# Feed-forward and output weights kept in SBUF for the 256-query passes of a two-layer attention and MLP kernel

## Chip, cores and metric

The kernel runs on one core of one Trainium2 chip. The metric is device time in microseconds (us) of one execution; the profile's span leaves out about 2 us of it.

## The reference, cut to what matters

```python
# S = 2048 tokens, D = 512, H = 32 heads of Dh = 16, F = 1792; bf16 in and out
def _A_ref(x, wqkv, wo):      # attention
    ...                       # q, k, v = x @ wqkv, by head
    scores = jnp.einsum("bhqd,bhkd->bhqk", q, k) * scale
    p = _softmax(scores, axis=-1)
    o = jnp.einsum("bhqk,bhkd->bhqd", p, v)
    return ... @ wo
def _B_ref(x, w1, w2):        # feed-forward
    h = _silu(jnp.einsum("bsd,df->bsf", x, w1))
    return jnp.einsum("bsf,fd->bsd", h, w2)

x = x + _A_ref(_layernorm(x), A_wqkv, A_wo)     # layer 0
x = x + _B_ref(_layernorm(x), B_w1, B_w2)
x = x + _A_ref(_layernorm(x), A_wqkv, A_wo)     # layer 1, the same weights
x = x + _B_ref(_layernorm(x), B_w1, B_w2)
```

Both layers use the same weights. `w1` is 1.8 MB (14 tiles of 128 KB), `wo` is 0.5 MB, `w2` is 1.8 MB and stays in SBUF throughout.

## The kernel before

The foreground is attention: scores on TensorE, exponentials mostly on ScalarE (a fourth of the blocks on VectorE and GpSimd instead), and their product with V on TensorE. Everything else (projections, layer norm, feed-forward) is cut into small pieces of "background", which a planner places at build time wherever its own model of the engines says TensorE has room. So TensorE's program is a fixed order in which background matmuls stand between score matmuls. If a background matmul waits, the scores behind it wait, and then the exponentials wait.

Queries go in passes. Layer 0 has four passes of 512 queries (`L, u` = 0, 0 to 3). Layer 1 has two passes of 512 (1, 0 and 1, 1) and four of 256 (1, 2 to 1, 5); the code calls the latter halved. The feed-forward of a pass runs in the background of the next one. The last one, of (1, 5), runs alone at the end and is called the tail.

Every load goes to one DMA queue, that of SyncE (SP), in program order. An instruction there that waits for a buffer or for its input holds back all that follow (below, a transpose that waited 3.4 us for its input held back a weight tile):

```python
def load(out, in_):
    nc.sync.dma_start(out, in_)
    if bg.model:
        bg.model.dma(1)               # charges the planner's model of the queue
...
w1pool = ctx.enter_context(tc.tile_pool(name="w1pool", bufs=3))
...
class W1:                             # one per pass: streams w1, two tiles ahead
    def __init__(self):
        self.tiles = {}
        for ft in range(2):
            self.load(ft)
    def load(self, ft):
        if ft < FT:                   # FT = 14
            self.tiles[ft] = w1pool.tile([P, CT, P], BF16, name="w1", tag="w1")
            load(self.tiles[ft][:], B_w1.rearrange(...)[:, :, ft * P : (ft + 1) * P])
    def get(self, ft):
        self.load(ft + 2)
        return self.tiles.pop(ft)
...
def h_pair(w1, ft, fT, i):            # 256-query passes: two tiles into one PSUM bank
    for k in range(2):
        yield part(pe=0.43, held=k > 0)
        if k == 0:
            ps = bank("h_ps")
        w = w1.get(ft + k)
        for ct in range(CT):
            nc.tensor.matmul(ps[...], lhsT=w[:, ct, :], rhs=fT[:, i : i + 2, ct, :], ...)
...
def load_wo():                        # wo shares the buffer of the hidden activations
    wo[0] = hpool.tile([P, FT, 512], BF16, name="wo", tag="hT")
    load(wo[0][:, 0:CT, :], A_wo.rearrange("(ct p) e -> p ct e", p=P))
...
def ffn(L, u):
    ...
    w1 = W1()
    yield part(need=("fT", L, u))     # fT: the normalized input, transposed by DMA
    hT = hpool.tile([P, FT, 512], BF16, name="hT", tag="hT")
    ...                               # h = silu(fT x w1) into hT, then hT x w2 into x
    load_wo()                         # for the next output projection
```

The output weights are thus loaded again after every feed-forward, because the hidden activations `hT` overwrite them, and the load can start only when the last reader of `hT` has finished. Shortly before the tail, `load_w1_tail` puts all 14 tiles of `w1` into slots that are free by then.

The softmax here doesn't subtract the row's maximum and nothing guards it: scores larger than these inputs give would overflow.

Of the kernel before, what the change touches and what calls it, by code (L numbers as in the profile page):

```python
# [20 lines left out]
BF16 = mybir.dt.bfloat16  # L21
# [206 lines left out]
def kernel(  # L228
# [10 lines left out]
    nc = tc.nc  # L239
# [4 lines left out]
    P = 128  # L244
# [3 lines left out]
    CT = D // P  # L248
    NC = S // 512
    FT = F // P  # L250
    NG = H // 8
    NKT = S // P
# [22 lines left out]
    ORDER = (*range(1, NG), 0)  # L275
# [14 lines left out]
    def halved(L, u):  # L290
        return L == 1 and u >= 2
# [17 lines left out]
    w1pool = ctx.enter_context(tc.tile_pool(name="w1pool", bufs=3))  # L309
# [9 lines left out]
    wo = {}  # L319
# [13 lines left out]
# [3 lines that stand above are left out]
            bg.model.dma(1)  # L336
# [42 lines left out]
    partial = {}  # L379

    def kslot(n, shape, dtype, name):

        return kpool.tile(shape, dtype, name=name, tag=f"K{n}")

    def xslot(n, name):

        return xtpool.tile([P, 4, CT, P], BF16, name=name, tag=f"X{n}")
# [252 lines left out]
    def load_wo():  # L640

        wo[0] = hpool.tile([P, FT, 512], BF16, name="wo", tag="hT")
        load(wo[0][:, 0:CT, :], A_wo.rearrange("(ct p) e -> p ct e", p=P))
# [37 lines left out]
        tt = 4 * c + i  # L681
        load(of[tt * P : (tt + 1) * P, :] if L == 1 else x1[c][:, i, :], x_sb[c][:, i, :])

    class W1:


        def __init__(self):
            self.tiles = {}
            for ft in range(2):
                self.load(ft)  # L690

        def load(self, ft):
            if ft < FT:
                self.tiles[ft] = w1pool.tile([P, CT, P], BF16, name="w1", tag="w1")
                load(
                    self.tiles[ft][:],
                    B_w1.rearrange("(ct p) f -> p ct f", p=P)[:, :, ft * P : (ft + 1) * P],
                )

        def get(self, ft):  # L700
            self.load(ft + 2)
            return self.tiles.pop(ft)

    def h_whole(w1, ft, fT):
        w = w1.get(ft)
        return (yield from mm4("h_ps", lambda ct: w[:, ct, :], lambda ct: fT[:, :, ct, :], out=0))

    def h_pair(w1, ft, fT, i):

        for k in range(2):  # L710
            yield part(pe=0.43, held=k > 0)
            if k == 0:
                ps = bank("h_ps")
            w = w1.get(ft + k)
            for ct in range(CT):
                nc.tensor.matmul(  # L716
                    ps[:, 256 * k : 256 * (k + 1)].rearrange("p (t q) -> p t q", q=P),
                    lhsT=w[:, ct, :],
                    rhs=fT[:, i : i + 2, ct, :],
                    start=(ct == 0),  # L720
                    stop=(ct == CT - 1),
                )
        yield part(0, held=True)
        return ps

    def ffn(L, u):
        c, tiles = tiles_of(L, u)
        if (L, u) < (1, 3):
            nxt = (c + 1) % NC
            load_x(nxt, x1[nxt] if (L, u) >= (0, NC - 1) else None)  # L730
        w1 = W1()
        yield part(need=("fT", L, u))
        fT = fTs.pop((L, u))
        hT = hpool.tile([P, FT, 512], BF16, name="hT", tag="hT")
        n = 2 if halved(L, u) else 1
        for ft in range(0, FT, n):
            if n == 1:
                h_ps = yield from h_whole(w1, ft, fT)
            else:
                h_ps = yield from h_pair(w1, ft, fT, tiles[0])  # L740
            t_sb = tpool.tile([P, 512], FP32, name="t_sb", tag="t")
            silu_tanh(h_ps, t_sb[:])
            yield part(0.6, held=True)
            silu_mul(
                hT[:, ft : ft + n, 0 : 512 // n],
                *(x.rearrange("p (n q) -> p n q", n=n) for x in (h_ps, t_sb[:])),
            )
        for k, i in enumerate(tiles):
            yield part(pe=0.43)
            y_ps = bank("f_ps")  # L750
            for ft in range(FT):
                nc.tensor.matmul(  # L752
                    y_ps,
                    lhsT=hT[:, ft, k * P : (k + 1) * P],
                    rhs=w2_sb[:, ft, :],
                    start=(ft == 0),
                    stop=(ft == FT - 1),
                )
                if ft % 2 == 1 and ft < FT - 1:
                    yield part(pe=0.43, held=True)  # L760
            yield part(0.6, held=True)
            ffn_out(L, c, i, y_ps)
            if L == 0 and i % 2 == 1:
                bg.add_side(None, ln_pair(c, i - 1))
        if L == 0:
            bg.add_side(("ln", 1, c), ln_attn(1, c))
        load_wo()

    def run(gen):

# [10 lines left out]
        for i in range(n):  # L781
            nc.tensor.matmul(ps, lhsT=ident[:], rhs=w_qkv[:, i % CT, 0:D], start=True, stop=True)  # L782

    w1_tail = {}

    def load_w1_tail():

        w1 = B_w1.rearrange("(ct p) f -> p ct f", p=P)
        rest = xslot(3, "w1_rest")
        for n in range(4):  # L790
            if n < 3:
                some = kslot(1 + n, [P, CT, 512], BF16, "w1_tail")
                nc.sync.dma_start(some[:], w1[:, :, 512 * n : 512 * (n + 1)])
            for ft in range(4 * n, min(4 * n + 4, FT)):
                if n < 3:
                    w1_tail[ft] = some[:, :, P * (ft % 4) : P * (ft % 4 + 1)]
                else:
                    w1_tail[ft] = rest[:, ft % 4, :, :]
                    nc.sync.dma_start(w1_tail[ft], w1[:, :, P * ft : P * (ft + 1)])

    def tail(L, u):

        c, tiles = tiles_of(L, u)
        aT = xslot(2, "aT")
        fT = xslot(L, "fT")
        ts = kslot(4, [P, 4, 256], FP32, "t_tail")
        LAG = 3
        COPY = (nc.vector.tensor_copy, nc.scalar.copy)

        def turn_tile(src, dst, copy):  # L810
            t_ps = bank("t_ps", BF16)[:, 0:512]
            for ct in range(CT):
                nc.tensor.transpose(  # L813
                    t_ps[:, ct * P : (ct + 1) * P], src[:, ct * P : (ct + 1) * P], ident[:, :]
                )
            copy(out=dst.rearrange("p c q -> p (c q)"), in_=t_ps)  # L816

        for n in range(2):
            turn_tile(attn[L, u][:, n, :], aT[:, n, :, :], COPY[n])
        for n, i in enumerate(tiles):  # L820
            run(out_add(c, i, aT[:, n, :, :]))
        warm(8)
        mv, rstd = run(ln_stats(c, tiles))
        for n, i in enumerate(tiles):
            xn = ln_apply(c, i, mv[:, n, :], rstd[:, n, :])
            turn_tile(xn, fT[:, n, :, :], COPY[1 - n])
            if n == 0:
                warm(2)

        hT = hpool.tile([P, FT, 512], BF16, name="hT", tag="hT")  # L830
        f_ps = [bank("f_ps") for _ in range(2)]

        def f_part(n, ft):
            nc.tensor.matmul(  # L834
                f_ps[n],
                lhsT=hT[:, ft, n * P : (n + 1) * P],
                rhs=w2_sb[:, ft, :],
                start=(ft == 0),
                stop=(ft == FT - 1),
            )  # L840

        for k in range(FT):
            h_ps = bank("h_ps")[:, 0:256]
            for ct in range(CT):
                nc.tensor.matmul(  # L845
                    h_ps.rearrange("p (t q) -> p t q", q=P),
                    lhsT=w1_tail[k][:, ct, :],
                    rhs=fT[:, 0:2, ct, :],
                    start=(ct == 0),
                    stop=(ct == CT - 1),  # L850
                )
            t_sb = ts[:, k % 4, :]
            silu_tanh(h_ps, t_sb)
            silu_mul(hT[:, k, 0:256], h_ps, t_sb)
            if k >= LAG:
                for n in range(2):
                    f_part(n, k - LAG)
        for n, i in enumerate(tiles):
            for ft in range(FT - LAG, FT):
                f_part(n, ft)  # L860
            ffn_out(L, c, i, f_ps[n])
# [9 lines left out]
    for g in range(NG):  # L871
        mine = [r for r in runs if r[3] == g]
        n = 0
# [24 lines left out]
    steps, pv_steps = plan()  # L898
    pv_left = {}
    for ts in pv_steps.values():  # L900
        t, k = ts[0]
        key = steps[t][0][k][0:5]
# [240 lines left out]
    with tc.manual_schedule(  # L1143
# [68 lines left out]
        for t in range(1, len(steps)):  # L1212
# [3 lines left out]
                if qc == 0:  # L1216
                    bg.ensure(("k", L, kt // 4, g))
            L, qc, pi, g, par, kt, j = a_blks[0]
            if t == len(steps) - 3 * NKT:
                load_w1_tail()  # L1220
            if kt == kts_of[L, qc, pi, g, par][0]:
                for Lq, c, gq, n in q_next.get((L, qc, pi, g, par), []):
                    bg.add(("q", Lq, c, gq, n), proj_q(Lq, c, gq), first=True)
# [17 lines left out]
            if t < D_LEAD:  # L1241
                p = p_pre[:, 3 * t + 1 : 3 * t + 4, :]
                parts = [p[:, 0:n1, :], p[:, n1 : n1 + 2, :]]
            elif n1 == 1:
                p = ppool.tile([P, 3, 512], BF16, name="p_sb", tag="p")
# [25 lines left out]
            if n1 == 2 and d_blks:  # L1271
                if t > 5 and m.free <= m.pe and bg.idle():
                    n = int((m.sd - m.pe - 2 * m.SWITCH) / m.GROUP)
# [6 lines left out]
            if not busy and m.fill_fits(FILL):  # L1280
                n = fill(FILL)
# [6 lines left out]
        t = len(steps) + 1  # L1288
# [40 lines left out]
```

## Time and profile before

| | before |
|---|---|
| median, 4 runs | 1580.38 us (1574.95 to 1582.19) |
| ScalarE (ACT) busy | 1512.2 of 1578.7 us |
| TensorE (PE) busy | 1465.1 us |
| HBM read | 33.29 MB |

The engine table of the profile of before: per engine, busy time, share of the span and instructions.

```profile
span 1578.7 us, 39884 instructions
...
PE 1465.1 (93%) x15947; PEld 536.1 (34%) x16056; DVE 1034.8 (66%) x1714; ACT 1512.2 (96%) x2185; POOL 1141.8 (72%) x1245
```

ScalarE is the bound. The Trainium skill, "Perfetto Trace Analysis", section "Identifying the Most-Contended Engine", says that for ScalarE the occupancy is also a fair measure of the distance to the roofline, and that a busy share of TensorE is not. The next view agrees: for over a millisecond ScalarE has next to no gap, while VectorE and GpSimd have slack. So the question is where its 66.5 us of idle time lie. This is the view by stretches of before (from and to, length, then busy time and instructions of each engine, granted TensorE clock, DMA share, GB/s). The bounds are start-up, middle, the stretch with the 256-query passes, and the tail.

```profile
core 0: us, PE busy (x) PEld busy (x) DVE busy (x) ACT busy (x) POOL busy (x), PEclk, DMA share, GB/s
0.00:100.00 100.00, 86.76 (x681) 28.61 (x689) 76.63 (x144) 86.74 (x125) 62.28 (x98) 0.98 0.28 77
100.00:1250.00 1150.00, 1091.98 (x10702) 363.59 (x10774) 778.71 (x1258) 1146.76 (x1657) 877.64 (x935) 1.00 0.15 33
1250.00:1549.87 299.87, 264.91 (x4422) 131.34 (x4447) 166.69 (x283) 272.15 (x390) 200.57 (x211) 0.93 0.23 51
1549.87:1579.00 29.13, 21.42 (x146) 12.59 (x148) 12.79 (x30) 6.54 (x16) 1.33 (x3) 0.94 0.03 10
```

Length less ScalarE busy gives idle time: 13.3, 3.2, 27.7 and 22.6 us. The third stretch stands out, and so does its clock of 0.93. What TensorE waited for there is the view of waits of before, cut to TensorE and this stretch (who <- for what: us in total, times, longest us):

```profile
PE y_ps L486 <- DMA wo<-in_A_wo_dram: 6.0, 2, 3.1
PE h_ps L716 <- DMA w_23318<-in_B_w_dram: 5.1, 1, 5.1
...
PE h_ps L716 <- DMA w_25071<-in_B_w_dram: 3.2, 1, 3.2
PE h_ps L716 <- DMA w_27182<-in_B_w_dram: 2.8, 1, 2.8
...
PE h_ps L716 <- DMA w_23626<-in_B_w_dram: 1.7, 1, 1.7
PE h_ps L716 <- DMA w_25379<-in_B_w_dram: 1.7, 1, 1.7
PE h_ps L716 <- DMA w_27490<-in_B_w_dram: 1.6, 1, 1.6
PE h_ps L716 <- DMA fT<-xn: 1.2, 1, 1.2
```

There are eight waits for weights of over 1 us, 22.1 us in sum: twice for `wo`, and in each of three passes for two tiles of `w1`. `wo` is late because it waits for its buffer: it was issued 1.3 us after the last matmul that read `hT`, and took 3.8 and 4.0 us to land. The tiles are late because of their place in the queue. The timeline of the DMA queue in before, around the longest wait (start, length, what was issued, how often), shows it:

```profile
1306.01 0.44 SPq L334 DMA_DIRECT2D w_22849<-in_B_w_dram  x1
1306.49 0.51 SPq L334 DMA_DIRECT2D w_22851<-in_B_w_dram  x1
1307.10 2.54 SPq L329 DMA_TRANSPOSE fT<-xn  x2
1309.75 1.69 SPq L329 DMA_TRANSPOSE ot<-oT  x1
1313.06 5.45 SPq L533 DMA_DIRECT2D QT<-q  x8
1318.63 1.19 SPq L329 DMA_TRANSPOSE ot<-oT  x1
1319.86 0.58 SPq L334 DMA_DIRECT2D w_23318<-in_B_w_dram  x1
...
1334.41 1.19 SPq L329 DMA_TRANSPOSE ot<-oT  x1
1335.69 0.53 SPq L334 DMA_DIRECT2D w_23626<-in_B_w_dram  x1
```

Tiles 1 and 2 are issued in time. Tile 3 (`w_23318`) stands behind eight query copies and two attention transposes and is issued at 1319.86; TensorE has stood still since 1317.45 and goes on at 1322.5. An issued tile of this size lands in 2.2 to 3.7 us in this stretch.

In a gap, or soon after it, the clock falls too. In the longest wait it fell at 1320.6, about 3 us into the gap. The view by stretches of before, for 9 us ahead of that wait and for the 6.8 us in which the clock was low:

```profile
1308.00:1317.00 9.00, 8.64 (x160) 4.54 (x156) 5.64 (x10) 9.00 (x15) 7.15 (x8) 1.00 0.64 89
1320.60:1327.40 6.80, 4.89 (x51) 2.55 (x52) 1.63 (x3) 2.52 (x4) 1.44 (x2) 0.50 0.43 96
```

A score matmul of 256 columns took 403 ns in the second stretch, against 271 from 1290 to 1317 us.

### The profile page before, as it was taken

What the parts mean: (1) busy time and instruction counts of PE and PEld (TensorE: products, weight loads), DVE (VectorE), ACT (ScalarE), POOL (GpSimd) and SP (SyncE); (2) the same over time, 40 slices, a digit from 0 to 9 for tenths busy, and PEclk for the clock granted to TensorE, in tenths of its full rate; (3) what the DMA queues carried; (4) which work ended last, traced back from release to release, by engine and by line L of the source; (5) the groups of instructions that cost most, each with busy time, mean ns of one, the idle gap of its engine ahead of it and who ended that gap; (6) DMA issues with size and microseconds to landing.
All of it is one profiled execution on the core that took longest, in us unless ns stands there. A gap on an engine that the chain in (4) does not pass through costs nothing. (4 is left out here: it accounts for less than half of the span.)

```text
span 1578.7 us, 39884 instructions
## 1 busy us (share of the span) xinstructions
PE 1465.1 (93%) x15947; PEld 536.1 (34%) x16056; DVE 1034.8 (66%) x1714; ACT 1512.2 (96%) x2185; POOL 1141.8 (72%) x1245
## 2 busy tenths in 40 slices
PE   7999999899989999899998999999998987889997
PEld 3222332233223333233332323322344444444444
DVE  6877676667766667666676677766676555555553
ACT  6999999999999999999999999999999988889994
POOL 2888777678867788678876777777787765667761
PEclk9999999999999999999999999999999999999999
DMA  4100022111220202201111010120122113121410
GB/s 140 31 24 2 5 38 65 28 34 25 51 55 15 46 14 53 49 18 41 34 39 31 11 32 13 43 51 24 36 51 50 24 31 79 34 61 30 91 40 19
DMA packets 168250, 61.51 MB, mean 39 GB/s; under 512 B 145536, under 2 KB 167552, under 8 KB 168064
## 3 DMA queue, kind: packets, MB, share of 16 engines
q1 hardware_dynamic: 168064, 58.96, 16.3%
q8 instruction: 125, 2.05, 0.5%
q14 instruction: 61, 0.50, 0.1%
HBM read 33.29 MB, written 4.19 MB: 24 GB/s over the span
## 5 line engine op out<-in xcount | busy, mean ns | idle before, releaser
L1186 ACT ACTIVATE p_sb<-s_ps 128x512 bf16<-128x512 f32 x2026 | 1467.9, 1107 | 12.6 <-PE d_ps L928 11.9
L1095 DVE TENSOR_SCALAR d_y<-d_ps 128x512 uint16<-128x512 f32 x1012 | 698.2, 690 | 463.5 <-PE d_ps L928 409.9
L928 PE MATMUL s_ps<-QT,KT 32*128 32x512 bf16 (+1 forms) x3852 | 641.3, 339 | 49.1 <-ACT p_sb L1186 35.3
L928 PEld LDWEIGHTS <-KT 32*128 32x128 bf16 x5120 | 199.9, 91 | 606.0 <-issue 564.9
L928 PE MATMUL d_ps<-QT,KT 32*128 32x512 bf16 (+1 forms) x1268 | 392.5, 342 | 3.1 <-DVE d_y L1095 2.5
L964 PE MATMUL o_ps<-p_sb,VA 128*32 128x512 bf16 (+1 forms) x3807 | 315.2, 346 | 7.0 <-ACT p_sb L1186 1.1
L964 PEld LDWEIGHTS <-VA 128*32 128x32 bf16 x5120 | 121.2, 96 | 138.0 <-issue 105.5
L964 PE MATMUL o_ps<-d_y,VA 128*32 128x512 f16 (+1 forms) x1268 | 154.1, 338 | 0.0
L964 PEld LDWEIGHTS <-VB 128*32 128x32 f16 x2536 | 99.6, 99 | 42.6 <-issue 0.5
L665 ACT ACTIVATE t_sb<-h_ps 128x512 f32<-128x512 f32 x105 | 90.9, 865 | 19.9 <-PE h_ps L716 16.7
L752 PE MATMUL f_ps<-w_sb,hT 128*128 128x512 bf16 x370 | 103.3, 384 | 5.7 <-issue 5.0
L668 DVE SCALAR_TENSOR_TENSOR hT<-t_sb,h_ps 128x512 bf16<-128x512 f32 x105 | 71.8, 684 | 20.0 <-ACT t_sb L665 19.0
L964 PE MATMUL o_ps<-w_qkv,zero 128*32 128x512 bf16 (+1 forms) x1356 | 73.3, 335 | 0.0
L1075 DVE CAST oT<-o_ps 128x512 bf16<-128x512 f32 (+1 forms) x80 | 45.9, 574 | 7.7 <-PE o_ps L964 7.7
L752 PEld LDWEIGHTS <-hT 128*128 128x128 bf16 x420 | 31.4, 98 | 48.4 <-issue 26.2
L419 DVE BATCH_NORM_STATS2 st<-x 128x6 f32<-128x512 bf16 x64 | 43.6, 681 | 2.0 <-DMA x<-in_A_x_dram 2.0
L430 DVE TENSOR_SCALAR xn<-x,mv,rstd 128x513 bf16<-128x513 bf16 x64 | 40.7, 650 | 2.9 <-POOL rstd L424 1.7
L964 PEld LDWEIGHTS <-zero 128*32 128x32 bf16 x1356 | 28.0, 95 | 27.1 <-issue 20.0
L486 PE MATMUL q_ps<-xnT,w_qkv 128*128 128x512 bf16 x136 | 35.9, 382 | 0.4 <-DVE q L531 0.2
L486 PE MATMUL k_ps<-xnT,w_qkv 128*128 128x512 bf16 x128 | 35.2, 386 | 1.0 <-DVE xnT L1164 0.6
L627 POOL TENSOR_TENSOR attn<-ot,rec 128x128 bf16<-128x128 bf16 (+1 forms) x61 | 31.1, 509 | 6.1 <-DVE rec L620 6.0
L486 PE MATMUL v_ps<-w_qkv,xnT 128*128 128x512 bf16 x112 | 33.0, 382 | 1.4 <-issue 0.6
(2355 smaller groups left out, 2089.5 us busy)
## 6 DMA issues: line engine op xcount, KB each, us to landing
wo<-in_A_wo_dram SPq DMA_DIRECT2D x10, 512.0 KB, 3.9
QT<-q SPq DMA_DIRECT2D x240, 16.0 KB, 1.8
x<-in_A_x_dram SPq DMA_DIRECT2D x7, 512.0 KB, 4.4
out_dram<-x SPq DMA_DIRECT2D x16, 128.0 KB, 1.8
w_sb<-in_B_w_dram SPq DMA_DIRECT2D x1, 1792.0 KB, 13.9
w_qkv<-in_A_wqkv_dram SPq DMA_DIRECT2D x3, 512.0 KB, 7.5
w_tail<-in_B_w_dram SPq DMA_DIRECT2D x3, 512.0 KB, 6.3
ot<-oT SPq DMA_TRANSPOSE x61, 2.4
```

Source lines behind the costliest of these rows:

```text
L419: nc.vector.bn_stats(st[:], x_sb[c][:, i, :])
L430: nc.vector.tensor_scalar(out=wide[:].rearrange("p (a b) -> p a b", b=19), in0=x_wide[c][:, D * i : D * (i + 1) + 1], scalar1=mv[:, 0:1], ...
L486: nc.tensor.matmul(ps.rearrange("p (t q) -> p t q", q=P) if len(r.shape) == 3 else ps, lhsT=lhs(ct), rhs=r, start=(ct == 0), stop=(ct == C ...
L627: scale(out=attn[L, qc][:, 0:n, P * g : P * (g + 1)].rearrange("p t (j s) -> p t j s", s=32)[:, :, :, 16 * par : 16 * par + 16], in0=att[: ...
L665: nc.scalar.activation(t_sb, h_ps, ACT.Tanh, scale=0.5)
L668: nc.vector.scalar_tensor_tensor(out=out, in0=t_sb, scalar=1.0, in1=h_ps, op0=ALU.add, op1=ALU.mult)
L752: nc.tensor.matmul(y_ps, lhsT=hT[:, ft, k * P : (k + 1) * P], rhs=w2_sb[:, ft, :], start=(ft == 0), stop=(ft == FT - 1),)
L928: nc.tensor.matmul(out[:, P * len(q) * n : P * len(q) * (n + 1)], lhsT=KT[L, kts // 4][r, g, (kts % 4) * P : (kts % 4 + 1) * P], rhs=QT[g] ...
L964: nc.tensor.matmul(o_tiles[key][32 * j : 32 * j + 32, 0:w], lhsT=lhsT[k] if real else zero[:], rhs=rhs[:, w * k : w * (k + 1)], start=(n[j ...
L1075: nc.vector.tensor_copy(out=o, in_=o_tiles[key][:, 0 : o.shape[-1]])
L1095: nc.vector.tensor_scalar(out=pr["y"][:, len(pr["ds"]), :], in0=s_ps[:], scalar1=float(1024 * SCALE * math.log2(math.e)), scalar2=float(10 ...
L1186: nc.scalar.activation(p_sb, s_ps, ACT.Exp, bias=-SHIFT * math.log(2.0) + math.log(EXP_SUM), scale=float(SCALE),)
```

## The change

Its intent is to load `w1` once for the three 256-query passes in the background and for the tail, into slots that the earlier passes have left free; to put `wo` beside it in a buffer of its own; and, in the 512-query passes, to prefetch the first two tiles of the next pass at the end of this one.

```diff
+    def next_w1(L, u, ft):
+        if (L, u) < (1, 1) or ft + 2 < FT:
+            load_w1((ft + 2) % FT)              # wraps into the next pass
+        elif ft + 2 == FT:                      # the last two tiles stay in w1pool
+            for k in (FT - 2, FT - 1):
+                w1_here[k] = w1pool.tile([P, CT, P], BF16, name="w1", tag="w1")[:]
+                load(w1_here[k], ...)
+        return w1.pop(ft)
 ...
-            w = w1.get(ft + k)
+            w = ws[k]
 ...
-                h_ps = yield from h_pair(w1, ft, fT, tiles[0])
+                h_ps = yield from h_pair([w1_here[ft + k] for k in range(2)], fT, tiles[0])
 ...
-        load_wo()
+        if (L, u) < (1, 1):
+            load_wo()
 ...
+    def keep_w1():                              # tiles 0 to 11
+        for n in range(3):
+            some = kslot(1 + n, [P, CT, 512], BF16, "w1_here")[:]
+            load(some, B_w1.rearrange(...)[:, :, 512 * n : 512 * (n + 1)])
+            for k in range(4):
+                w1_here[4 * n + k] = some[:, :, P * k : P * (k + 1)]
+
+    def keep_wo():
+        wo[0] = xslot(3, "wo_here")[:].rearrange("p t c q -> p t (c q)")
+        load(wo[0], A_wo.rearrange("(ct p) e -> p ct e", p=P))
 ...
-            if t == len(steps) - 3 * NKT:
-                load_w1_tail()
+            if kt == 0 and (L, qc, pi, g, par) == (1, 2, 0, ORDER[1], 0):
+                assert not any(key[0:2] <= (1, 1) for key in partial)
+                keep_w1()
+            if kt == 0 and (L, qc, pi, g, par) == (1, 2, 0, ORDER[-1], 0):
+                keep_wo()
```

The planner charges fewer loads to its model of the queue, so it also places some background work of layer 1 a few steps away from where it was.

More of the change, by code (lines that the diff above doesn't have):

```diff
@@ L682, in ffn_out, with load_w1, h_whole, h_pair @@
         load(of[tt * P : (tt + 1) * P, :] if L == 1 else x1[c][:, i, :], x_sb[c][:, i, :])
-    class W1:
-        def __init__(self):
-            self.tiles = {}
-            for ft in range(2):
-                self.load(ft)
-        def load(self, ft):
-            if ft < FT:
-                self.tiles[ft] = w1pool.tile([P, CT, P], BF16, name="w1", tag="w1")
-                load(
-                    self.tiles[ft][:],
-                    B_w1.rearrange("(ct p) f -> p ct f", p=P)[:, :, ft * P : (ft + 1) * P],
-                )
-        def get(self, ft):
-            self.load(ft + 2)
-            return self.tiles.pop(ft)
-    def h_whole(w1, ft, fT):
-        w = w1.get(ft)
+    w1 = {}
+    def load_w1(ft):
+        w1[ft] = w1pool.tile([P, CT, P], BF16, name="w1", tag="w1")[:]
+        load(w1[ft], B_w1.rearrange("(ct p) f -> p ct f", p=P)[:, :, ft * P : (ft + 1) * P])
+    def next_w1(L, u, ft):
[4 more added lines that the diff above has]
+                w1_here[k] = w1pool.tile([P, CT, P], BF16, name="w1", tag="w1")[:]
+                load(w1_here[k], B_w1.rearrange("(ct p) f -> p ct f", p=P)[:, :, k * P : (k + 1) * P])
+        return w1.pop(ft)
+    def h_whole(w, fT):
         return (yield from mm4("h_ps", lambda ct: w[:, ct, :], lambda ct: fT[:, :, ct, :], out=0))
-    def h_pair(w1, ft, fT, i):
+    def h_pair(ws, fT, i):
         for k in range(2):
@@ L730, in ffn @@
             load_x(nxt, x1[nxt] if (L, u) >= (0, NC - 1) else None)
-        w1 = W1()
+        if (L, u) == (0, 0):
+            load_w1(0)
+            load_w1(1)
         yield part(need=("fT", L, u))
@@ L737, in ffn @@
             if n == 1:
-                h_ps = yield from h_whole(w1, ft, fT)
+                h_ps = yield from h_whole(next_w1(L, u, ft), fT)
             else:
-                h_ps = yield from h_pair(w1, ft, fT, tiles[0])
+                h_ps = yield from h_pair([w1_here[ft + k] for k in range(2)], fT, tiles[0])
             t_sb = tpool.tile([P, 512], FP32, name="t_sb", tag="t")
@@ L782, in warm @@
             nc.tensor.matmul(ps, lhsT=ident[:], rhs=w_qkv[:, i % CT, 0:D], start=True, stop=True)
-    w1_tail = {}
-    def load_w1_tail():
-        w1 = B_w1.rearrange("(ct p) f -> p ct f", p=P)
-        rest = xslot(3, "w1_rest")
-        for n in range(4):
-            if n < 3:
-                some = kslot(1 + n, [P, CT, 512], BF16, "w1_tail")
-                nc.sync.dma_start(some[:], w1[:, :, 512 * n : 512 * (n + 1)])
-            for ft in range(4 * n, min(4 * n + 4, FT)):
-                if n < 3:
-                    w1_tail[ft] = some[:, :, P * (ft % 4) : P * (ft % 4 + 1)]
-                else:
-                    w1_tail[ft] = rest[:, ft % 4, :, :]
-                    nc.sync.dma_start(w1_tail[ft], w1[:, :, P * ft : P * (ft + 1)])
+    w1_here = {}
+    def keep_w1():
+        for n in range(3):
+            some = kslot(1 + n, [P, CT, 512], BF16, "w1_here")[:]
+            load(some, B_w1.rearrange("(ct p) f -> p ct f", p=P)[:, :, 512 * n : 512 * (n + 1)])
+            for k in range(4):
[3 more added lines that the diff above has]
+        load(wo[0], A_wo.rearrange("(ct p) e -> p ct e", p=P))
     def tail(L, u):
@@ L846, in tail @@
                     h_ps.rearrange("p (t q) -> p t q", q=P),
-                    lhsT=w1_tail[k][:, ct, :],
+                    lhsT=w1_here[k][:, ct, :],
                     rhs=fT[:, 0:2, ct, :],
```

## The prediction

> **What bounds the kernel now.** ScalarE. The engine table gives it 1512.2 us busy of a 1578.7 us span (96%); 1467.9 us are the softmax exponentials (table of groups). The change neither adds nor removes a ScalarE instruction, so only its 66.5 us of idle time can shrink. By stretches: first 100 us 13; 100 to 1250 us 3.2 (1.8 and 1.4, at 447 and 636); 1250 to 1550 us 27.9 (PE clock 0.93); tail 22. The third stretch holds the three 256-query passes of layer 1 that run beside attention.
>
> **What ends those waits.** There TensorE waits for first feed-forward weight tiles (5.1, 3.2, 2.8, 1.7, 1.7, 1.6 us), for the output weights twice (6.0 us in sum) and once for a transposed activation (1.2). The DMA queue's timeline shows why: it is in order, a weight tile sits behind eight query copies (5 us) and attention transposes, and the output weights are issued only once the hidden buffer is free, about 1 us before they are needed, and take 3.9 us to land. Each TensorE gap is followed by 3.4 or 6.8 us at granted clock 0.50; a score matmul then takes 403 ns against 270. This agrees with the Trainium skill, "TensorE: Matmul & The Clock Gate", Part 1 (half rate after an idle window of about 3.4 us, windows free-running), except that gaps of only 1.2 us were followed by it here. ScalarE loses gap and cold aftermath: 4.5 + 4.2 us at the output-weight waits, 5.6 + 1.4 + 3.3 + 1.9 + 3.3 + 1.8 us at the weight-tile waits: 26 us. 1.1 us belongs to the transposed activation.
>
> **What the change does.** The 14 tiles are loaded once before the first 256-query pass, the output weights into a buffer of their own, both long before use. 42 tile loads (5.5 MB) and three output-weight loads (1.6 MB) go; HBM reads fall from 33.3 to about 26.2 MB. The DMA saving itself is worth nothing. What counts is that all eight weight waits go, with their cold clock. Elsewhere the first two tiles are prefetched at the end of the previous chunk; but the two layer-0 waits are for the third tile, which keeps its place behind query copies and an attention transpose: I expect both to stay. PE's order is unchanged until the first output projection of the halved passes; later work moves by a few steps.
>
> **Critical path.** All 26 us are idle time of the bounding engine, so they should come off one for one. I give back about 3 us: the passes start earlier and may wait 1 to 2 us for transposed activations, which share the queue, with some cold clock.
>
> **Prediction: 1557.5 us**, 8 in 10 between 1552 and 1567. Faster by over 2% 0.05 (needs 31.6 us, more than all waits there), within 2% 0.93, slower 0.02.
>
> **Right if:** ScalarE busy stays near 1512 us and idles about 43; from 1250 to 1550 it is busy over 290 us and PE's clock is 0.98 or more; no wait for either weight after 1250; at least six of the eight half-speed intervals there go; the waits at 447 and 636 stay.
> **Wrong step if:** the weight waits are gone but ScalarE idles as before: then transposes or the plan took their place.
>
> **What would make it wrong:** a planner that, with cheaper DMA, packs background matmuls so that exponentials wait; late transposes in all three passes; run-to-run spread (1575 to 1582 before).

## The result, and the profile after

| | before | after |
|---|---|---|
| median | 1580.38 us (4 runs, 1574.95 to 1582.19) | 1554.09 us (4 runs, 1553.61 to 1557.71) |
| ratio, 95% interval | | 0.9844 (0.9816 to 0.9873) |
| ScalarE busy / idle | 1512.2 / 66.5 us | 1510.2 / 41.6 us |
| HBM read | 33.29 MB | 26.21 MB |

The change is 1.6% faster, inside the 2% that count as the same class. The engine table of the profile after:

```profile
span 1551.8 us, 39817 instructions
...
PE 1456.6 (94%) x15947; PEld 535.6 (35%) x16056; DVE 1036.6 (67%) x1714; ACT 1510.2 (97%) x2185; POOL 1143.1 (74%) x1245
```

The same four stretches of after; the tail now begins at 1523.16.

```profile
0.00:100.00 100.00, 87.00 (x661) 28.93 (x668) 75.27 (x142) 84.29 (x122) 60.65 (x97) 0.97 0.29 77
100.00:1250.00 1150.00, 1091.21 (x10680) 362.93 (x10752) 779.05 (x1259) 1146.79 (x1657) 878.15 (x933) 1.00 0.16 35
1250.00:1523.16 273.16, 256.98 (x4463) 131.11 (x4489) 169.44 (x285) 272.52 (x394) 202.99 (x214) 1.00 0.11 22
1523.16:1552.00 28.84, 21.41 (x146) 12.60 (x148) 12.79 (x30) 6.55 (x16) 1.33 (x3) 0.92 0.03 10
```

ScalarE idles 15.7, 3.2, 0.6 and 22.3 us. The third stretch does about the same ScalarE work (394 instructions and 272.5 us, against 390 and 272.2) in 26.7 us less; the clock is at 1.00. The middle has not gained anything. The start is 2.4 us worse, of which more below. The waits of TensorE in the third stretch of after:

```profile
PE s_ps L924 <- ACT p_sb L1182: 7.9, 20, 0.4
...
PE h_ps L711 <- DMA fT<-xn: 1.4, 1, 1.4
```

No wait for weights is left. The one wait for a DMA is the transposed activation, as before. At the top TensorE now waits for ScalarE, which is how it looks when ScalarE is the bound. The queue of after, where tile 3 was late (the timeline of the DMA queue):

```profile
1295.84 7.75 SPq L533 DMA_DIRECT2D QT<-q  x11
1303.63 0.58 SPq L334 DMA_DIRECT2D x<-x_3_113  x1
1304.33 2.55 SPq L329 DMA_TRANSPOSE fT<-xn  x2
1306.98 8.44 SPq L329 DMA_TRANSPOSE ot<-oT  x2
```

The weights are no longer in it; they were issued at 1163.58, over 140 us before the first pass that uses them.

### The profile page after: what moved, and what is told of

Its sections match the earlier page's. It is cut to its first block, busy times and chain, and to the rows that moved or that the text cites. A ratio compares the mean times of both kernels' runs of the same rounds, so it can differ in the third digit from the quotient of the medians. Undisturbed runs are those within 1.5% of the kernel's fastest.

```text
span 1551.8 us, 39817 instructions
## 1 busy us (share of the span) xinstructions
PE 1456.6 (94%) x15947; PEld 535.6 (35%) x16056; DVE 1036.6 (67%) x1714; ACT 1510.2 (97%) x2185; POOL 1143.1 (74%) x1245
## 3 DMA queue, kind: packets, MB, share of 16 engines
HBM read 26.21 MB, written 4.19 MB: 20 GB/s over the span
## 5 line engine op out<-in xcount | busy, mean ns | idle before, releaser
L960 PEld LDWEIGHTS <-zero 128*32 128x32 bf16 x1356 | 28.1, 95 | 27.1 <-issue 20.0
```

The costliest lines, as they stand in the source:

```text
L960: nc.tensor.matmul(o_tiles[key][32 * j : 32 * j + 32, 0:w], lhsT=lhsT[k] if real else zero[:], rhs=rhs[:, w * k : w * (k + 1)], start=(n[j ...
```

## The experiments

The theory of the prediction, "waits": the gain is the eight waits for weights and the cold clock behind them, at one us per us because they were ScalarE's idle time. There are two rivals. "Traffic": the gain is the 7.1 MB that are no longer loaded. "Plan": the gain is the other placement of background work that the planner made because it charged fewer loads. The first four runs shared seven runs of before, with a median of 1579.33 us (1577.80 to 1587.33).

| kernel | `w1` kept | `wo` kept | bytes | plan | median us | ratio to before (95%) | ScalarE idle, third stretch |
|---|---|---|---|---|---|---|---|
| before | no | no | 33.3 MB | before | 1579.33 | | 27.7 |
| prefetch_only | no | no | 33.3 MB | after | 1576.39 | 0.9964 (0.9929 to 0.9999) | 21.2 |
| wo_only | no | yes | 31.7 MB | before | 1571.21 | 0.9941 (0.9905 to 0.9977) | 16.7 |
| w1_only | yes | no | 27.8 MB | after | 1562.63 | 0.9887 (0.9852 to 0.9922) | 10.5 |
| traffic_back | yes | yes | 33.3 MB | before | 1555.18 | 0.9825 (0.9781 to 0.9870) | 0.4 |
| after (its own rounds) | yes | yes | 26.2 MB | after | 1554.09 | 0.9844 (0.9816 to 0.9873) | 0.6 |

"Plan" says whose order of instructions ScalarE, VectorE and GpSimd have in the compiled program; it was compared instruction by instruction. (TensorE's was not. In the traces, 35 of ScalarE's 2185 instructions stand at another place in the one plan than in the other.) The idle time is from the view by stretches, from 1250 us to the start of the tail in each profile.

### w1_only: the output weights loaded again after every pass

```diff
-        if (L, u) < (1, 1):
-            load_wo()
+        load_wo()
...
-            if kt == 0 and (L, qc, pi, g, par) == (1, 2, 0, ORDER[-1], 0):
-                keep_wo()
```

> The changed kernel with the output weights loaded again after every pass, as before; the 14 first feed-forward tiles stay resident. Order of work on ScalarE, VectorE and GpSimd is that of the changed kernel. Waits theory (each removed TensorE wait for weights, with its cold clock, is ScalarE time): the two output-weight waits near 1283 and 1369 us come back and nothing else, 1554 + 8.7 = about 1563 us. Traffic theory (the gain is the 7.1 MB of loads no longer made): 1.6 MB come back, 1554 + 6 = 1560. Plan theory (the gain is the other order of background work): 1554. The returned waits in the trace tell the first two apart, more than the time.

Measured: 1562.63 us (1562.37 to 1566.45, four runs). The waits of TensorE for DMA in the third stretch of w1_only:

```profile
...
PE y_ps L486 <- DMA wo<-in_A_wo_dram: 5.6, 2, 2.8
PE h_ps L711 <- DMA fT<-xn: 1.9, 1, 1.9
```

The two waits for `wo` are back, and no others for weights. ScalarE idles 10.5 us there, 8.3 of it at those two waits. The waits theory said 1563. The 1560 of the traffic theory is too near to be excluded by the time alone.

### wo_only: the kernel before with the output weights kept

```diff
-        load_wo()
+        if (L, u) < (1, 1):
+            load_wo()
+        if (L, u) == (1, LAST - 1):      # the slot of the tail's last two tiles is taken
+            for k in (FT - 2, FT - 1):
+                w1.load(k)
+                w1_tail[k] = w1.tiles.pop(k)[:]
...
+            if kt == 0 and (L, qc, pi, g, par) == (1, 2, 0, ORDER[-1], 0):
+                keep_wo()
```

> The kernel before with the output weights kept in a buffer of their own from the first 256-query pass; the first feed-forward tiles are streamed as before. Order of work on ScalarE, VectorE and GpSimd is that of the kernel before. Waits theory: the six weight-tile waits of the 256-query passes stay (17.3 us of ScalarE idle time), the two output-weight waits go: 1580 - 8.7 = about 1571.5 us. Traffic theory: 1.6 of 7.1 MB gone, 1574. Plan theory: 1580.

Measured: 1571.21 us (1570.33 to 1575.68), and the view of TensorE's waits in the third stretch of wo_only, cut to those for DMA:

```profile
PE h_ps L716 <- DMA w<-in_B_w_dram: 16.5, 9, 5.7
PE h_ps L716 <- DMA fT<-xn: 1.0, 1, 1.0
```

The waits for `wo` are gone and those for `w1` remain (16.5 us, against 16.1 in the six large ones of before). By medians, keeping `w1` alone is worth 16.7 us and keeping `wo` alone 8.1; the sum, 24.8, is close to what both give together (26.3 in the first measurement, 24.2 for traffic_back in these rounds). The two halves add up, as they should if each takes away its own waits. The split is not quite clean: w1_only also has the other plan, which is tested next.

### prefetch_only: neither weight kept

```diff
-        if (L, u) < (1, 1) or ft + 2 < FT:
+        if (L, u) < (1, LAST - 1) or ft + 2 < FT:
             load_w1((ft + 2) % FT)
-        elif ft + 2 == FT:
-            ...                          # nothing stays
...
-            w = ws[k]
+            w = next_w1(L, u, ft + k)
...
-        if (L, u) < (1, 1):
-            load_wo()
+        load_wo()
...                                       # keep_w1, now with all 14 tiles, ahead of the tail as before
```

> Only the third part of the change: the first two tiles are prefetched across the passes, in the 256-query passes too; neither weight is kept. Order of work on ScalarE, VectorE and GpSimd is that of the changed kernel. Waits theory: the third and eleventh tiles still stand behind query copies and transposes in the DMA queue, and the output-weight waits stay: 1578 to 1581 us. Traffic theory: 1580. Plan theory: 1554.

Measured: 1576.39 us (1573.05 to 1577.15), 1.6 us below the expected range; the interval of the ratio ends just below 1. The other plan with the prefetch is thus worth about 3 us by the medians and 6 by the ratio (its interval goes from 0 to 11), not 26. Where these come from is visible: in this order the query copies no longer stand ahead of tile 3 of the first 256-query pass, and the longest wait for a tile is 2.9 us in place of 5.1 (it is now the fifth tile that waits there, not the third as expected). The waits as such remain, as the view of TensorE's waits of prefetch_only shows for the third stretch, cut to those for DMA:

```profile
PE h_ps L707 <- DMA w<-in_B_w_dram: 14.3, 9, 2.9
PE y_ps L486 <- DMA wo<-in_A_wo_dram: 5.1, 2, 2.6
PE h_ps L707 <- DMA fT<-xn: 2.0, 1, 2.0
```

### traffic_back: all the loads made, none waited for

The weights are kept as in the changed kernel, and the removed loads are put back at their places into buffers without a reader. (Space was short: one of the two buffers is an eighth smaller.)

```diff
+    unread = {1: dumpool.tile([P, CT, 112], BF16, name="unread1")[:]}
...
+            unread[0] = w1pool.tile([P, CT, P], BF16, name="unread0", tag="w1")[:]
...
             w = ws[k]
+            unread_w1(ft + k + 2)        # a load into unread[0] or unread[1]
...
+        if halved(L, u):
+            unread_w1(0)
+            unread_w1(1)
...
         if (L, u) < (1, 1):
             load_wo()
+        else:
+            ...                          # wo in four parts into the same two buffers
```

> The changed kernel with the removed loads put back at their old places in the queue, into two buffers that nobody reads (every second tile 7/8 as large for lack of space, so 97% of the bytes), and charged to the planner as before. Order of work on ScalarE, VectorE and GpSimd is exactly that of the kernel before. Only the waiting for them is gone. Waits theory: 1554 to 1557 us, no weight wait after 1250 us, HBM reads back near 33 MB. Traffic theory: about 1580. Plan theory: about 1580.

Measured: 1555.18 us (1550.73 to 1557.88). HBM reads are 33.34 MB, and the plan is that of before. The view by stretches of traffic_back for the third stretch:

```profile
1250.00:1526.75 276.75, 264.74 (x4555) 132.85 (x4545) 171.64 (x290) 276.39 (x400) 205.58 (x216) 1.00 0.23 48
```

The only wait of TensorE for DMA in that stretch, from the view of its waits:

```profile
PE h_ps L723 <- DMA fT<-xn: 1.1, 1, 1.1
```

The DMA share is 0.23, as in before, and ScalarE idles 0.4 us. Both rivals had said about 1580 for this run, so both fall: with all the bytes and the old plan, the gain is there once nobody waits. Together with prefetch_only (new plan, waits kept: 1576) this settles what the gain is made of.

### filler_before: the waits kept, the cold clock taken away

Idle-filling matmuls stand ahead of the matmuls that waited for weights, so that TensorE works while the load is on its way. The edit hits six of the eight: in the second pass (`u` = 3) its fillers stand at the third and the eleventh tile, where the waits were for the fifth and the thirteenth.

```diff
             w = w1.get(ft + k)
+            if ft + k == 2:
+                warm({2: 22, 3: 13, 4: 12}[u], ps)     # matmuls of 128x512, overwritten later
+            elif ft + k == 10:
+                warm(7, ps)
...                                       # and 13 ahead of the first y_ps of passes (1, 2) and (1, 3)
```

> The kernel before with idle-filling matmuls (7 to 22 of 128x512, 1.5 to 4.7 us) in front of each of the eight matmuls of the 256-query passes that waited for weights: the waits last as long, but TensorE works in them. Same order elsewhere. This takes away the cold clock alone. If the cold clock costs what the trace says beyond the waits themselves (26.0 us of ScalarE loss less 22.1 us of TensorE gaps): 1580 - 4 = 1576 us, with most of the half-speed intervals after 1250 us gone. If the cold clock costs much more than that (half of the 26 us): 1567. If it costs nothing: 1580.

Measured: 1575.06 us (1568.51 to 1578.54, six runs) beside 1579.32 of before (11 runs), ratio 0.9965 (0.9940 to 0.9990). The granted clock of the third stretch is 0.99, and one half-speed interval is left of eight. It follows the wait for the thirteenth tile of the second pass, 2.3 us, which the misplaced filler left; these are all the waits for weights that remain in the stretch:

```profile
PE h_ps L722 <- DMA w<-in_B_w_dram: 3.8, 6, 2.3
```

So the clock accounts for about 4 us by the medians, near the 3.9 us that the traces gave as ScalarE's loss beyond TensorE's gaps. That is probably too little: the fillers took 21.7 us and the remaining waits 3.8, so TensorE was held some 3 us longer than by the 22.1 us of waits in before. The two profiles differ by more (ScalarE idle 19.2 us in the stretch against 27.7). The size of this part is thus known only roughly, 4 to 8 us; most of the loss is the waits.

### third_early: the waits that were left in the 512-query passes

The changed kernel still waits for the third tile of a 512-query pass, because that tile keeps its place behind transposes and query copies. `w1pool` has a third slot that is free at the start of a pass.

```diff
-        if (L, u) < (1, 1) or ft + 2 < FT:
+        if ft == 0:
+            pass
+        elif (L, u) < (1, 1) or ft + 2 < FT:
             load_w1((ft + 2) % FT)
...
+        if not halved(L, u):
+            load_w1(2)                   # ahead of the wait for fT
         yield part(need=("fT", L, u))
```

It ran with the changed kernel beside it, twice:

> The changed kernel once more, to stand beside the next two runs in the same rounds: 1554 us.

> The changed kernel, with the third tile of each whole pass too loaded at the pass's start, ahead of the transposes and query copies in the queue, in the slot of the pool that is free then. Same bytes, no other order on ScalarE and TensorE. If the three waits left in the whole passes (0.7, 1.5 and 0.8 us of ScalarE idle time at 449, 637 and 1046 us) are queue position, they go: 1554 - 3 = 1551 us, and the half-speed interval at 1045 us goes. If they are landing time itself, or if the fourth tile then waits in its stead, 1553 to 1554.

Measured: 1547.38 us (1545.67 to 1553.76), against 1553.09 (1551.78 to 1556.51) of the changed kernel. The ratios to before are 0.9799 (0.9773 to 0.9824) and 0.9835 (0.9809 to 0.9861). The view by stretches of third_early, start-up and middle:

```profile
0.00:100.00 100.00, 87.27 (x687) 28.45 (x688) 76.59 (x144) 86.69 (x125) 62.23 (x98) 0.98 0.28 77
100.00:1250.00 1150.00, 1102.19 (x10821) 365.05 (x10820) 780.80 (x1261) 1149.78 (x1662) 880.04 (x937) 1.00 0.16 35
```

ScalarE idles 0.2 us in the middle, where after has 3.2: the waits were queue position. But the first 100 us are also 2.4 us better than in the two profiles of the changed kernel, although nothing differs there. So the pair ran again.

> The changed kernel again, beside the next. ScalarE busy in the first 100 us was 84.3 in both of its profiles, with a half-speed interval near 11 us, and 86.7 in that of third_early, without one; the instructions there are the same. If that is chance of the clock's windows, it falls out differently between runs: 1551 to 1554 us, and some profile of this kernel without the interval. If it belongs to the build, it is there again: 1553 to 1554.

> The same kernel as third_early. It came out 5.7 us below the changed kernel where the waits account for 3.0. If the other 2.4 to 2.7 us are the start's clock by chance: 1548 to 1551 us, with ScalarE idle between 100 and 1250 us again under 1 us (3.2 in the changed kernel). If the third tile's place is worth more than its waits: 1547 again, without a difference in the first 100 us.

Measured: 1552.89 us (1551.71 to 1554.92) for the changed kernel and 1550.38 us (1550.11 to 1550.58) for third_early_2, with ratios of 0.9833 and 0.9815 (0.9788 to 0.9842). The start fell the other way round. The first 100 us of after_third, by stretches:

```profile
0.00:100.00 100.00, 86.72 (x681) 28.66 (x689) 76.68 (x144) 86.80 (x125) 62.32 (x98) 0.98 0.27 77
```

and start-up and middle of third_early_2:

```profile
0.00:100.00 100.00, 86.46 (x661) 27.44 (x668) 74.89 (x141) 84.02 (x121) 60.29 (x96) 0.95 0.27 77
100.00:1250.00 1150.00, 1094.22 (x10726) 364.63 (x10799) 781.66 (x1262) 1150.00 (x1662) 880.37 (x937) 1.00 0.16 35
```

The middle of third_early_2 has no idle time at all (1150.00 of 1150), and its start has a half-speed interval of 6.8 us at 32 us that third_early had not. The start is chance between runs, not a property of the kernel; what decides it is not shown (the five times of third_early_2 lie within 0.5 us of each other, so it need not change from one execution to the next). The third tile's place takes away about 3 us of ScalarE's idle time (3.2 in after, 4.4 in after_third); that the two measurements, 5.7 and 2.5 us, are this plus and minus the start fits the profiles but rests on two pairs. third_early is the best version seen, 2.0% and 1.9% below before, so whether it crosses the 2% remains unclear.

## Why the prediction was right

- **The bound and the place of the loss.** ScalarE busy stayed (1510.2 us for 1512.2), and the stretch of the 256-query passes gave back 27.1 us of its 27.7 us of idle time. Shown by the two views by stretches. The spans of the two profiles differ by 26.9 us: 24.9 of idle time and 2.0 of busy time; why ScalarE was busy 2.0 us less was not looked into.
- **The cause.** All eight waits for weights went, and so did all eight half-speed intervals of the stretch (seven behind weight waits, one behind the wait for the transposed activation). That these waits, and neither the bytes nor the plan, are the gain is shown by traffic_back and prefetch_only; the two weights' shares, put at 17.3 and 8.7 us, came out at 16.7 and 8.1 (w1_only, wo_only).
- **HBM reads.** Predicted about 26.2 MB, measured 26.21.
- **What stays.** The waits at 447 and 636 us stayed (ScalarE gaps of 0.7 and 1.5 us at 449 and 637). A third gap, of 0.8 us at 1046, came in; the prediction had none there. Its tile landed at 1045.28. Prefetching two tiles across the passes therefore gained nothing in the middle: idle time 3.2 us before and after. third_early shows that the third tile was the one to move.
- **The size.** 1557.5 was predicted and 1554.1 measured. The mis-sized term is the "about 3 us" of giving back, for passes that might now wait for transposed activations with some cold clock: in the profile 0.6 us of ScalarE's time remained in the stretch. The total of idle time, predicted as about 43 us, is 41.6; it includes 2.4 us lost at the start by chance. That it came so near is thus partly luck: without the slow start it would have been about 39.
- **Three inexact statements.** "Each TensorE gap is followed by 3.4 or 6.8 us" at half speed was one too many: the stretch of before has nine gaps of over 1.2 us and eight intervals, and the gap of 1.7 us at 1336.5 has none. And the test "from 1250 to 1550 it is busy over 290 us" did not allow for the tail moving into that window: there it is busy 279 us, so the test as worded fails; measured to the tail's start, ScalarE is busy 272.5 of 273.2 us. "A weight tile sits behind eight query copies" holds for one of the six tiles; the others stood behind a transpose that waited for its input.

## What to carry to other kernels

A DMA wait counts for what it takes from the bounding engine, so add up that engine's gaps by their releasers, stretch by stretch, before asking how many bytes a change saves: here 7 MB less traffic at a DMA share of 0.23 was worth nothing measurable (ratios 0.9844 without it and 0.9825 with it, in different rounds), and eight waits of 1.6 to 5.1 us, with the low clock behind them, were worth about 26 us. Here a small load in a queue that issues in order was late because of what stood ahead of it, sometimes a single transpose whose input was not there yet; moving it up, or loading it once long before, took the wait away. When you test waits one by one, look up in the trace which instruction waits in each pass: here it was not the same tile in all three. When two builds differ by 2 to 3 us, look at the first 100 us before crediting the change.

## What the Trainium skill lacked or had wrong

- "TensorE: Matmul & The Clock Gate", Part 1 and "HAM oscillation": the page gives an idle window of about 3.4 us as what halves the clock, and as a rule no idle gaps over about 3.4 us. In these traces shorter gaps were enough: in or within 2 us of gaps of 1.2, 1.7, 2.9 and 3.1 us in before came 3.4 or 6.8 us at 0.50. But the same gaps did not always do it: 1.7 us (before, 1336.5) and 2.3 us (after, 635) had none after them. The page's note that the windows are free-running and vary by run agrees with this. The page also mentions a kernel in which frequent short idles do it, but it states no length and no probability for gaps under a window.
- The same page says that the slow start varies from run to run, puts its cost under 1% of a typical span and advises not to fit it. The size agrees: its variation moved ScalarE's busy time in the first 100 us between 86.8, 84.0 and, with 17 us at half speed in traffic_back, 81.8 us, that is 0.2 to 0.3% of the span. But it is as large as the gain under test in third_early, which the page does not warn of.
- "DMA: Bandwidth & Descriptors", "Anatomy of one DMA": a fixed cost of about 2.0 us plus bytes over 436 GB/s, fitted for DMAs that GpSimd issues. An estimate from it for a 128 KB tile is 2.3 us, and 2.2 to 2.7 us was usual for those that SyncE issued here. For 512 KB it gives 3.2 us; the output weights took a median of 3.9 us, the kept feed-forward weights, three issued together, 5.1 us.
- The pages give no figure that we found for how long the issuing queue is held. In the trace of before, eight query copies of 16 KB in a row held it for 4.9 to 5.9 us, and a DMA transpose for 1.2 us (median of 149). For the longest wait it was mainly this issue time of what stood ahead, and for the other tiles mainly a transpose's wait for its input (3.4 to 5.8 us), that made the tile late.
